# Where twelve table scatters and four operand subtractions stand in an attention stage with routing

## The chip, the cores and the metric

The kernel runs on one core of one Trainium2 chip. The metric is device time in microseconds (us), lower is better. The kernel before took 800.71 us, the median of three runs (800.22 to 800.90). One further execution was profiled; every row below comes from it.

## The reference

Four batches of 768 tokens go through attention with 8 heads of 64 dimensions. Six random projections give each query and key a bucket of 6 bits, and a query sees only keys of its own bucket; where there is none, the masked softmax is uniform. The result is a matrix of 3072 tokens by 512, which a router sends to one of eight experts each.

```python
scores = scale * np.matmul(q, k.transpose(0, 1, 3, 2))
scores = np.where(mask, scores, -1000000000.0)
attn = np.exp(scores - np.max(scores, axis=-1, keepdims=True))
attn = attn / (np.sum(attn, axis=-1, keepdims=True) + 1e-09)
x = np.matmul(attn, v)                       # then (3072, 512)
logits = x @ w_gate + modality_bias[modality_id]
e_idx = np.argmax(logits, axis=1)            # one expert a token
out[mask] = gate_w[mask, None] * (np.maximum(x[mask] @ w1[e], 0.0) @ w2[e])
```

## The kernel before, in words

Attention goes over 16 pairs of heads, four pairs to a batch, numbered 0 to 15. Within a pair there are six steps kt, one for each block of 128 keys. Products run as two float32r matmuls, on a high part and a low part of each operand. For a later pair i the copies `hx` (L161, ScalarE) are the high parts of q (x = 0) and k (x = 1), and one subtraction each (L163) makes the low parts: `b_0` of q and `b_1` of k, 128x768 each. k's low part is made by VectorE; q's is made by GpSimd (POOL), but by VectorE in pairs 9, 10, 13 and 14, which the line RELIEF lists:

```python
lo = nc.vector if i in RELIEF or (x == 1 and i > 1) else nc.gpsimd
```

Both are wanted about two pairs later. On VectorE one of them stands in the last step of pair i-3 or so, ahead of the last reduction of the row maxima (L232). What hangs on that reduction: the maximum `m` (L240, VectorE), its negative `nm` (L242, ScalarE), and its transpose on TensorE (L249), behind which all of TensorE's next work waits, since TensorE works in program order. The transposed maxima lie in PSUM tiles `psx`, of which there are two. VectorE gives one back when it has made `lone` (L252) from it, and then the bucket patterns of the next pair (L207) can be written into it.

GpSimd adds up the exponentials for the row sums: two adds of 128x768 (L302) for each step kt, once ScalarE's second exponential of the step (L299) is done. It also makes `va` (L258 to L260) from the values.

Once the four pairs of a batch are through, the next four pairs carry its routing in small pieces: logits, argmax (`oh`), the rank of each token among its expert's (`rk`), and so each token's row in a table in DRAM (`posi`, six columns of one int32, L615, VectorE). Six indirect DMAs issued by GpSimd (L619) then scatter the records (token, gate weight) of the batch's six token blocks into those rows of `tab`. `posi` is one buffer for all batches. For batch 0 the six scatters are issued in pair 7, for batch 1 in pair 11, for batch 2 in pair 14. Each is placed behind the latest add of GpSimd. In pair 14 the table is first read back (`etb`, L694) for two early expert slots.

Two strings of letters for each step (PLAN) say which piece comes next; TensorE's and SyncE's order is the program's, those of VectorE, ScalarE and GpSimd are made by a scheduler. After pair 15 comes the expert stage, whose work before 520 us belongs partly to the last batch.

Of the kernel before, what the change touches and what calls it, by code (L numbers as in the profile page):

```python
# [19 lines left out]
NT = S // 128  # L20
# [8 lines left out]
LAG = 3  # L29
XAT = (12, 6)  # L30
GAT = ((-13, -10, -7, -4), (-1, -1, -1, -1))
RELIEF = (9, 10, 13, 14)
UPTO = 12
PLAN = (
    "LvSPMSMSfMTfexyhk",
    "SMSMVfSMAAQTeyghk",
    "SMTSMSMlGEfxyk",
    "SMTSMSMAAFGEekk",
    "SMSMTSMgfExehk",
    "SMTSMTSMBAABFGFfFfggehkk",  # L40
)
FIN = (("G", "g", "h", "k"), ("FG", "f", "eE", "eE"))
AHEAD = 2
# [31 lines left out]
    }  # L75


def attention(ctx, actx, tc, a, x_d, route, setup, early_slots, early_tables, latest, adds, bias):
    nc = tc.nc
    v = a["v"]  # L80
    NPR = a.get("npair", NP)
# [6 lines left out]
    ps_x = ctx.enter_context(tc.tile_pool(name="ps_x", bufs=CFG["psx"], space=PSUM))  # L88
# [22 lines left out]
    def load_v(i):  # L111
        b, c = i // 4, i % 4
        t = st[i]
        t["v"] = ldv.tile([P, 2, NT, D], F32, name="vt")
        nc.sync.dma_start(out=t["v"], in_=v[b, 2 * c:2 * c + 2].rearrange("h (p t) d -> p h t d", t=NT))
# [318 lines left out]
    with tc.manual_schedule(engines={mybir.EngineType.PE, mybir.EngineType.SP}):  # L434
        load(1)
        load_v(0)
        load(2)
        load_v(1)
        first_scores = score(0)
        first()  # L440
        wg = sm.tile([P, 4, 8], F32, name="wg", bufs=1)
        nc.sync.dma_start(out=wg, in_=a["moe_w_gate"].rearrange("(c p) e -> p c e", p=P))
        gst = fconst.tile([P, 4, 32], F32, name="gst")
        nc.gpsimd.memset(gst, 0.0)
        nc.gpsimd.tensor_copy(out=gst[0:64, :, 0:8], in_=wg[0:64])
        nc.gpsimd.tensor_copy(out=gst[64:128, :, 16:24], in_=wg[64:128])
        ones = fconst.tile([P, 4, 32], F32, name="ones")
        nc.gpsimd.memset(ones, 0.0)
        for c in range(4):
            nc.gpsimd.memset(ones[:, c, c:c + 1], 1.0)  # L450
        setup()
        avs = weigh()
        fins = xs = ts = iter(())
        for i in range(NPR):
            late = []
            ss = score(i) if i else first_scores
            ms = maxp(i + 1, late) if i + 1 < NPR else iter(())
            last, ts = ts, prep(i + 2) if i + 2 < NPR else iter(())
            if i % 4 == 0 and i > 0:
                fins = finish(i // 4 - 1) if i < NPR - 4 else finish_last()  # L460
            for kt in range(NT):
                for c in (PLAN if i else PLAN0)[kt]:
                    if c == "S":
                        next(ss)
                    elif c == "M":
                        next(ms, None)
                    elif c == "T":
                        next(ts, None)
                    elif c == "P":
                        next(last, None)  # L470
                    elif c == "A":
                        next(avs)
                    elif c == "B":
                        if late:
                            late.pop(0)()
                    elif c == "v":
                        vadds(i)
                    elif c == "V":
                        vsums(i)
                    elif c == "Q":  # L480
                        if i > 0:
                            sums(i - 1)
                    elif c == "L":
                        if i + 3 < NPR:
                            load(i + 3)
                    elif c == "l":
                        if 0 < i < NPR - 1:
                            load_v(i + 1)
                    elif c in FIN[i >= NPR - 4][i % 4]:
                        with tc.issue_after(newest[0]):  # L490
                            next(fins, None)
                    elif c == "x" and i % 4 == 2 or c == "y" and i % 4 == 3:
                        if c == "x" and kt == 0 and i > 4:
                            xs = finish_x(i // 4 - 1, 0, NT)
                        next(xs, None)
                        next(xs, None)
        for _ in avs:
            pass
        sums(NPR - 1)
# [12 lines left out]
EARLYB = 2  # L512
# [17 lines left out]
def router(ctx, tc, a, x_d, tab):  # L530
# [43 lines left out]
            nc.gpsimd.tensor_copy(out=run[0], in_=base)  # L574
            nc.gpsimd.tensor_copy(out=recs[:, :, :, 0], in_=tok)

    scattered, latest, adds = [], [], []

    def route(b, lg, ps):
        l = lg  # L580
        m = wk.tile([P, NT], F32, name="rm")
        nc.vector.tensor_reduce(out=m, in_=l, axis=AX.X, op=ALU.max)
        d = wk.tile([P, NT, E], F32, name="rd")
        nc.vector.tensor_tensor(out=d, in0=l, in1=m.unsqueeze(2).broadcast_to([P, NT, E]), op=ALU.subtract)
        ex = wk.tile([P, NT, E], F32, name="rex")
        nc.scalar.activation(ex, d, AF.Exp)
        yield
        w = wk.tile([P, NT, E], F32, name="rw")
        nc.vector.scalar_tensor_tensor(out=w, in0=d, scalar=0.0, in1=rev.unsqueeze(1).broadcast_to([P, NT, E]), op0=ALU.is_ge, op1=ALU.mult)
        wm = wk.tile([P, NT], F32, name="rwm")  # L590
        nc.vector.tensor_reduce(out=wm, in_=w, axis=AX.X, op=ALU.max)
        oh = wk.tile([P, NT, E], BF16, name="oh")
        nc.vector.tensor_tensor(out=oh, in0=w, in1=wm.unsqueeze(2).broadcast_to([P, NT, E]), op=ALU.is_equal)
        yield
        pp = ps.tile([P, HALF], F32, name="psx")
        for j in range(NT):
            lhs = tri if j == 0 else onesb
            nc.tensor.matmul(pp[:, j * E:NT * E], lhs, oh[:, 0:NT - j].rearrange("p t e -> p (t e)"), start=(j == 0), stop=False, skip_group_check=True)
        for j in range(NT):
            nc.tensor.matmul(pp[:, 64:64 + E], onesb, oh[:, j], start=False, stop=(j == NT - 1), skip_group_check=True)  # L600
        rk = wk.tile([P, NT, E], F32, name="rk")
        nc.vector.tensor_tensor(out=rk, in0=pp[:, 0:NT * E].rearrange("p (t e) -> p t e", e=E), in1=run[b % 2].unsqueeze(1).broadcast_to([P, NT, E]), op=ALU.add)
        nc.vector.tensor_tensor(out=run[(b + 1) % 2], in0=run[b % 2], in1=pp[:, 64:64 + E], op=ALU.add)
        yield
        rec = recs[:, b]
        sm = wk.tile([P, NT], F32, name="rsum")
        nc.vector.tensor_reduce(out=sm, in_=ex, axis=AX.X, op=ALU.add)
        nc.vector.tensor_scalar(out=sm, in0=sm, scalar1=1e-9, scalar2=None, op0=ALU.add)
        nc.vector.reciprocal(rec[:, :, 1].bitcast(F32), sm)
        yield  # L610
        nc.vector.tensor_tensor(out=rk, in0=rk, in1=oh, op=ALU.mult)
        pos = wk.tile([P, NT], F32, name="pos")
        nc.vector.tensor_reduce(out=pos, in_=rk, axis=AX.X, op=ALU.add)
        posi = wk.tile([P, NT], I32, name="posi")
        nc.vector.tensor_copy(out=posi, in_=pos)  # L615
        yield
        for t in range(NT):
            with tc.issue_after(latest[0]) if b < B - 1 else nullcontext():
                ins = nc.gpsimd.indirect_dma_start(out=tab, out_offset=bass.IndirectOffsetOnAxis(ap=posi[:, t:t + 1], axis=0), in_=rec[:, t], in_offset=None).ins  # L619
            for other in scattered:  # L620
                tc.declare_no_dep(ins, other, reason="every token has its own row of the table")
            scattered.append(ins)
            if b < B - 1:
                yield

# [62 lines left out]
    ete = const.tile([P, EARLY, TG, 2], I32, name="ete")  # L688

    def early_tables():  # L690
        for j in range(EARLY):
            o = nc.values_load(eslot[0:1, 1, j:j + 1], engines=[mybir.EngineType.SP], min_val=0, max_val=DUMMY,
                               skip_runtime_bounds_check_because="the on-chip slot table ends with the dummy block")
            nc.sync.dma_start(out=etb[:, j], in_=tab[bass.ds(o, TS), :].rearrange("(p a) w -> p a w", a=TG))  # L694
# [24 lines left out]
        nc.vector.tensor_copy(out=tot[:, 2:3], in_=over[:, 0:1])  # L719
        return big, sml, tot  # L720

    return route, early_slots, early_tables, (eslot, etb, ete), late_slots, setup, latest, adds, bias


def experts(ctx, tc, a, x_d, tab, out, ps_x, ident, first, adds):
# [247 lines left out]
def body(tc, a, out):  # L973
# [1 line left out]
    x_d = tc.dram_tile([N + 1, DM], F32, name="x_d")  # L975
    tab = tc.dram_tile([DUMMY + TS, 2], I32, name="tab")
    with ExitStack() as ctx, ExitStack() as actx:
        route, early_slots, early_tables, early_tiles, late_slots, setup, latest, adds, bias = router(ctx, tc, a, x_d, tab)
        finish, finish_x, ps_x, ident = attention(ctx, actx, tc, a, x_d, route, setup, early_slots, early_tables, latest, adds, bias)
        actx.close()  # L980
        runner, tabs, conditional = experts(ctx, tc, a, x_d, tab, out, ps_x, ident, early_tiles, adds)
        r = runner()
# [38 lines left out]
```

## Time and profile before

| what | value |
|---|---|
| timed runs | 800.22, 800.71, 800.90 us |
| profiled execution | 798.11 us, its span 796.3 us |
| TensorE busy | 748.0 us, 94% of the span |
| VectorE, ScalarE, GpSimd busy | 505.0, 413.6, 438.9 us |
| attention, pairs 0 to 15 | until about 485 us |

The span is what the profile shows between the first and the last instruction; the rest, 1.8 us, lies around it. A row of the timeline has start and duration in us, engine, line, operation, what is written and read, its shape, how often it came in a row, and in brackets how long the engine sat idle before it and who ended that. A duration contains what an instruction waits inside itself, for a port for instance. A row of the windows has the stretch, its length, busy time and number of instructions of each engine, TensorE's granted clock (1.00 is 2.4 GHz, 0.50 is 1.2 GHz), the DMA share and GB/s.

### The profile page before, as it was taken

The numbers are of one execution on the slowest core, as the hardware profiler recorded it, in microseconds if no ns is written. First come the engines' busy times: TensorE is split into PE (matmuls) and PEld (weight loads), VectorE is DVE, ScalarE is ACT, GpSimd is POOL, SyncE is SP. The second block draws the span as 40 slices with busy tenths as digits, with TensorE's granted clock in tenths as the row PEclk, the third lists the DMA queues.
The fourth block names the chain that finished last, engine by engine and source line by source line (L and its number), as shares of the span: only waits on it lengthen the run. The fifth ranks groups of instructions, "written<-read, shape, count | busy, mean of one in ns | idle before, by whom it ended". The sixth has DMA issues, their size and how long they took to land.

```text
span 796.3 us, 11626 instructions
## 1 busy us (share of the span) xinstructions
PE 748.0 (94%) x4060; PEld 522.6 (66%) x4060; DVE 505.0 (63%) x839; ACT 413.6 (52%) x730; POOL 438.9 (55%) x321
## 2 busy tenths in 40 slices
PE   4799999999999999997899899999999999999996
PEld 1555556566655566654555555888888888888885
DVE  5777677587787769778769859764244342752422
ACT  3566666666557566664446455324253334633323
POOL 7198988788779978697857694034220204202002
PEclk9999999999999999999999999999999999999999
DMA  6665544254347524465310276466443535833321
GB/s 204 154 179 159 159 119 129 71 159 113 103 123 160 136 83 117 126 153 121 93 48 14 63 161 218 155 90 229 132 159 86 165 101 173 278 134 123 130 54 60
DMA packets 59572, 104.24 MB, mean 131 GB/s; under 512 B 9709, under 2 KB 30829, under 8 KB 59504
## 3 DMA queue, kind: packets, MB, share of 16 engines
q1 hardware_dynamic: 53424, 88.23, 40.0%
q0 software_dynamic: 4928, 13.14, 5.1%
q10 hardware_dynamic: 1152, 2.03, 0.9%
q8 instruction: 34, 0.56, 0.3%
q14 instruction: 34, 0.28, 0.1%
HBM read 59.89 MB, written 13.33 MB: 92 GB/s over the span
## 4 chain that ended last, share of the span: by engine, by line
PE 68%; DVE 11%; issue 10%; ACT 6%; DMA 2%; SPq 1%; POOL 1%; POOLq 0%; ACTq 0%; DVEq 0%
PE psu L326 12%; PE pss L280 8%; PE pss L281 6%; PE hps L812 5%; PE hps L813 5%; PE hps L811 5%; PE yps L857 4%; PE yps L855 4%; PE yps L856 4%; PE psm L224 4%; ACT pb L292 3%; PE psm L230 2%; DVE mx L226 1%; DVE a_0g L251 1%; PE psx L344 1%
## 5 line engine op out<-in xcount | busy, mean ns | idle before, releaser
L302 POOL TENSOR_TENSOR sp<-sp,pb 128x768 f32<-128x768 f32 x124 | 230.9, 1887 | 35.6 <-ACT pb L299 32.2
L292 ACT ACTIVATE pb<-pss 128x512 f32<-128x512 f32 x192 | 113.8, 598 | 104.8 <-PE pss L281 89.4
L226 DVE TENSOR_REDUCE mx<-psm 128x1 f32<-128x512 f32 x192 | 130.7, 687 | 55.2 <-PE psm L224 54.2
L764 DVE TENSOR_TENSOR w<-raw,w 128x1024 fp32r<-128x1024 f32 x64 | 79.5, 1249 | 94.9 <-ACT w L762 66.5
L326 PE MATMUL psu<-pb,vt 128*64 128x512 f32 (+1 forms) x768 | 134.4, 492 | 0.0
L762 ACT CAST w<-raw 128x1024 fp32r<-128x1024 f32 x64 | 66.9, 1050 | 73.8 <-PE yps L857 62.4
L326 PEld LDWEIGHTS psu<-pb,vt 128*64 128x64 f32 x768 | 50.8, 136 | 69.1 <-issue 58.8
L782 POOL DMA_INDIRECT xg<-x_d,tb x18 | 21.9, 1219 | 117.7 <-DMA tb<-tab 113.4
L280 PE MATMUL pss<-a_0g 128*128 128x512 f32 x192 | 80.4, 419 | 3.5 <-ACT pb L292 2.2
L855 PE MATMUL yps<-w,hl 128*128 128x512 f32 x208 | 82.7, 398 | 0.0
L302 POOL TENSOR_TENSOR sp<-pb,pb 128x768 f32<-128x768 f32 x31 | 58.9, 1918 | 41.0 <-ACT pb L299 40.9
L857 PE MATMUL yps<-w,hh 128*128 128x512 f32 x208 | 81.3, 391 | 0.0
L856 PE MATMUL yps<-w,hh 128*128 128x512 f32 x208 | 81.0, 389 | 0.0
L812 PE MATMUL hps<-xl,w 128*128 128x512 f32 x192 | 74.8, 390 | 1.4 <-DVE xl L801 1.4
L811 PE MATMUL hps<-xh,w 128*128 128x512 f32 x192 | 75.5, 393 | 0.0
L813 PE MATMUL hps<-xh,w 128*128 128x512 f32 x192 | 74.8, 390 | 0.0
L232 DVE TENSOR_REDUCE mx<-psm 128x2 f32<-128x512 f32 x96 | 66.1, 689 | 9.6 <-PE psm L230 7.4
L280 PE MATMUL pss<-a_1g 128*128 128x512 f32 x192 | 68.3, 356 | 3.7 <-ACT pb L299 3.4
L817 ACT ACTIVATE hh<-hps 128x512 fp32r<-128x512 f32 x48 | 28.7, 598 | 74.0 <-PE hps L813 71.8
L281 PE MATMUL pss<-b_0g 128*128 128x512 f32 x192 | 65.9, 343 | 0.0
L281 PE MATMUL pss<-b_1g 128*128 128x512 f32 x192 | 65.7, 342 | 0.0
L818 DVE SCALAR_TENSOR_TENSOR hl<-hps,hh 128x512 fp32r<-128x512 f32 x48 | 33.0, 688 | 51.1 <-ACT hh L817 50.5
(203 smaller groups left out, 1374.3 us busy)
## 6 DMA issues: line engine op xcount, KB each, us to landing
raw<-moe_w SPq DMA_DIRECT2D x64, 512.0 KB
xt<-qk SPq DMA_DIRECT2D x31, 384.0 KB
vt<-v SPq DMA_DIRECT2D x16, 384.0 KB
a_0g<-hx SPq DMA_DIRECT2D x30, 192.0 KB
a_1g<-hx SPq DMA_DIRECT2D x30, 192.0 KB
x_d<-xs SPq DMA_DIRECT2D x18, 256.0 KB
b_1g<-a_1g SPq DMA_DIRECT2D x17, 192.0 KB
b_0g<-a_0g SPq DMA_DIRECT2D x17, 192.0 KB
```

The costliest lines, as they stand in the source:

```text
L226: newest[:] = [nc.vector.tensor_reduce(out=mx[:, qt + j, 1 - h, 0:1], in_=mp, axis=AX.X, op=ALU.max).ins]
L280: nc.tensor.matmul(out, t["s1"][h][:, ks], t["m1"][h][:, cs], start=True, stop=False)
L281: nc.tensor.matmul(out, t["s2"][h][:, ks], t["m2"][h][:, cs], start=False, stop=True)
L292: nc.scalar.activation(t["pb"][kt][:, h, 0:MAIN], sp, AF.Exp, scale=0.125)
L302: add = (nc.vector if h and i in CFG["spd"] else nc.gpsimd).tensor_tensor(out=t["sp"][:, h], in0=(t["pb"][0] if kt == 1 else t["sp"])[:, h ...
L326: nc.tensor.matmul(t["u"][part][64 * h:64 * h + 64, 0:w], t["v"][:, h, kt], t["pb"][kt][:, h, COLS[part]], start=False, stop=(kt == NT - 1 ...
L811: nc.tensor.matmul(hps, lo[:, c, fs], xh[:, c], start=(c == 0), stop=False)
L812: nc.tensor.matmul(hps, hi[:, c, fs], xl[:, c], start=False, stop=False)
L813: nc.tensor.matmul(hps, hi[:, c, fs], xh[:, c], start=False, stop=(c == 3))
L855: nc.tensor.matmul(yps[g], hl[fc][:, gs], hi[:, fb], start=(fc == 0), stop=False)
L856: nc.tensor.matmul(yps[g], hh[fc][:, gs], lo[:, fb], start=False, stop=False)
L857: nc.tensor.matmul(yps[g], hh[fc][:, gs], hi[:, fb], start=False, stop=(fc == 7))
```

## The change

RELIEF is emptied, so that GpSimd makes q's low part in pairs 9, 10, 13 and 14 too. The six scatters of batches 0 and 1 are no longer issued by the routing itself. They are put on a list, and a new letter s in the plan issues one: in steps kt 1, 4 and, for the last pair of a batch only, 5; not in the third pair of a batch (i % 4 is 2). For batch 0 that is kt 4 and 5 of pair 7, kt 1 and 4 of pair 8, kt 1 and 4 of pair 9; for batch 1 the same in pairs 11, 12 and 13. Batches 2 and 3 are left as they were.

```diff
-RELIEF = (9, 10, 13, 14)
+RELIEF = ()
 PLAN = (
     "LvSPMSMSfMTfexyhk",
-    "SMSMVfSMAAQTeyghk",
+    "SMSMVfSMAAQTesyghk",
...
-    "SMSMTSMgfExehk",
-    "SMTSMTSMBAABFGFfFfggehkk",
+    "SMSMTSMgfExeshk",
+    "SMTSMTSMBAABFGFfFfggehksk",
 )
...
+                    elif c == "s":
+                        if later and i % 4 != 2 and (kt < NT - 1 or i % 4 == 3):
+                            later.pop(0)()
...
-        for t in range(NT):
+
+        def put(t):
             with tc.issue_after(latest[0]) if b < B - 1 else nullcontext():
                 ins = nc.gpsimd.indirect_dma_start(out=tab, ...).ins
...
+        puts = [partial(put, t) for t in range(NT)]
+        if b < EARLYB:
+            later.extend(puts)
+            return
+        for p in puts:
+            p()
             if b < B - 1:
                 yield
...
     def early_tables():
+        assert not later
```

The order of TensorE and of SyncE is the same before and after. On the others the pieces below show what stands where.

GpSimd, before, from the second step of pair 11 to the first of pair 12. `pb_...` are the five buffers of exponentials, `tab<-recs,posi` is a scatter:

```order
L302 TENSOR_TENSOR sp<-sp,pb_163 128x768 x2
L619 DMA tab<-recs,posi 25088x2
L302 TENSOR_TENSOR sp<-sp,pb_164 128x768 x2
L619 DMA tab<-recs,posi 25088x2 x2
L302 TENSOR_TENSOR sp<-sp,pb_160 128x768 x2
L619 DMA tab<-recs,posi 25088x2
L302 TENSOR_TENSOR sp<-sp,pb_161 128x768 x2
L619 DMA tab<-recs,posi 25088x2
L302 TENSOR_TENSOR sp<-pb_162,pb_163 128x768 x2
```

The same stretch in the changed kernel:

```order
L302 TENSOR_TENSOR sp<-sp,pb_163 128x768 x2
L302 TENSOR_TENSOR sp<-sp,pb_164 128x768 x2
L302 TENSOR_TENSOR sp<-sp,pb_160 128x768 x2
L623 DMA tab<-recs,posi 25088x2
L163 TENSOR_TENSOR b_0g_115<-xt,hx 128x768
L302 TENSOR_TENSOR sp<-sp,pb_161 128x768 x2
L623 DMA tab<-recs,posi 25088x2
L302 TENSOR_TENSOR sp<-pb_162,pb_163 128x768 x2
```

The scatters ahead of and between the adds of kt 2 to 4 are gone; the first one now stands behind the add of kt 4 (`pb_160`), and behind it q's low part of pair 14.

VectorE, before, in the last step of pair 11 and on to the row sums of pair 12 (L349), the two low parts of pair 14:

```order
L163 TENSOR_TENSOR b_0g_115<-xt,hx 128x768
L232 TENSOR_REDUCE mx<-psm 128x2
L251 SCALAR_TENSOR_TENSOR a_0g_120<-psx,a_0g_120 64x512
L240 TENSOR_REDUCE m_3823<-mx 128x4
L251 SCALAR_TENSOR_TENSOR a_1g_121<-psx,a_1g_121 64x512
L252 TENSOR_SCALAR lone<-psx 128x512
...
L232 TENSOR_REDUCE mx<-psm 128x2
L163 TENSOR_TENSOR b_1g_116<-xt,hx 128x768
L349 TENSOR_TENSOR gs<-gs,psx 128x384
```

The same in the changed kernel:

```order
L163 TENSOR_TENSOR b_1g_116<-xt,hx 128x768
L232 TENSOR_REDUCE mx<-psm 128x2
L251 SCALAR_TENSOR_TENSOR a_0g_120<-psx,a_0g_120 64x512
L240 TENSOR_REDUCE m_3819<-mx 128x4
L251 SCALAR_TENSOR_TENSOR a_1g_121<-psx,a_1g_121 64x512
L252 TENSOR_SCALAR lone<-psx 128x512
...
L232 TENSOR_REDUCE mx<-psm 128x2
L349 TENSOR_TENSOR gs<-gs,psx 128x384
```

The place ahead of L232 is not emptied: k's low part has moved up into it, and the one ahead of L349 is gone. It is the same in pairs 6, 7 and 10.

VectorE, before, at the end of pair 13, where the table rows of batch 2 (`posi`) are made:

```order
L226 TENSOR_REDUCE mx<-psm 128x1
L615 CAST posi<-pos 128x6
L232 TENSOR_REDUCE mx<-psm 128x2
L251 SCALAR_TENSOR_TENSOR a_0g_113<-psx,a_0g_113 64x512
L240 TENSOR_REDUCE m_4433<-mx 128x4
L251 SCALAR_TENSOR_TENSOR a_1g_114<-psx,a_1g_114 64x512
L252 TENSOR_SCALAR lone<-psx 128x512
```

The same in the changed kernel:

```order
L226 TENSOR_REDUCE mx<-psm 128x1
L232 TENSOR_REDUCE mx<-psm 128x2
L251 SCALAR_TENSOR_TENSOR a_0g_113<-psx,a_0g_113 64x512
L240 TENSOR_REDUCE m_4433<-mx 128x4
L251 SCALAR_TENSOR_TENSOR a_1g_114<-psx,a_1g_114 64x512
L618 CAST posi<-pos 128x6
L252 TENSOR_SCALAR lone<-psx 128x512
```

The cast stands four places later, just ahead of the `lone` that gives a `psx` tile back. It overwrites the `posi` that batch 1's scatters read, so it waits until those have landed; the last of them is now issued in step 4 of pair 13.

## Rows read from the trace of the kernel before

**Rows 1.** Page, part 1: busy time, share of the span, instructions of each engine.

```profile
PE 748.0 (94%) x4060; PEld 522.6 (66%) x4060; DVE 505.0 (63%) x839; ACT 413.6 (52%) x730; POOL 438.9 (55%) x321
```

**Rows 2.** Windows: from pair 7's row sums to pair 8's; pair 11's to 12's.

```profile
228.70:255.70 27.00, 26.42 (x160) 16.50 (x158) 20.75 (x35) 17.71 (x35) 25.61 (x18) 1.00 0.71 159
...
340.90:372.90 32.00, 27.76 (x160) 17.55 (x158) 25.29 (x35) 17.38 (x34) 26.99 (x20) 0.95 0.55 134
```

**Rows 3.** Timeline of TensorE: four instructions in pairs 6, 11, 12 and 13.

```profile
219.96 0.37 PE L249 MATMUL psx<-identr,nm 128*128 128x128 f32 x2 [1.15 <-ACT nm L242]
...
363.58 0.37 PE L249 MATMUL psx<-identr,nm 128*128 128x128 f32 x2 [3.79 <-DMA b_0g<-hx]
...
397.78 0.32 PE L207 MATMUL psx<-bits,pat 128*128 128x384 bf16 x1 [1.28 <-DVE gl L386]
...
426.66 0.34 PE L207 MATMUL psx<-bits,pat 128*128 128x384 bf16 x1
```

**Rows 4.** Timeline of ScalarE in the last steps of pair 11.

```profile
354.27 0.60 ACT L299 ACTIVATE pb<-pss 128x512 f32<-128x512 f32 x1
...
363.11 0.41 ACT L242 ACTIVATE nm<-m 128x256 fp32r<-128x256 f32 x1 [4.67 <-DVE m L240]
```

**Rows 5.** Timeline of VectorE: the subtraction ahead of L232 in pairs 6, 7, 11, 12.

```profile
215.53 2.40 DVE L163 TENSOR_TENSOR b_0g<-xt,hx 128x768 fp32r<-128x768 f32 x1
...
244.15 0.95 DVE L163 TENSOR_TENSOR b_0g<-xt,hx 128x768 fp32r<-128x768 f32 x1
...
356.53 5.03 DVE L163 TENSOR_TENSOR b_0g<-xt,hx 128x768 fp32r<-128x768 f32 x1
...
390.38 1.04 DVE L163 TENSOR_TENSOR b_1g<-xt,hx 128x768 fp32r<-128x768 f32 x1
```

**Rows 6.** Timeline of GpSimd at those four places and in pair 13.

```profile
213.49 3.62 POOL L302 TENSOR_TENSOR sp<-sp,pb 128x768 f32<-128x768 f32 x2 [1.77 <-ACT pb L299]
...
244.20 1.73 POOL L619 DMA_INDIRECT tab<-recs,posi  x1 [0.31 <-issue]
...
356.19 0.96 POOL L619 DMA_INDIRECT tab<-recs,posi  x1 [0.30 <-issue]
357.17 3.57 POOL L302 TENSOR_TENSOR sp<-sp,pb 128x768 f32<-128x768 f32 x2
...
388.76 4.33 POOL L302 TENSOR_TENSOR sp<-sp,pb 128x768 f32<-128x768 f32 x2 [3.55 <-ACT pb L299]
393.06 1.81 POOL L163 TENSOR_TENSOR b_0g<-xt,hx 128x768 fp32r<-128x768 f32 x1
394.83 3.58 POOL L302 TENSOR_TENSOR sp<-sp,pb 128x768 f32<-128x768 f32 x2
...
421.21 7.21 POOL L302 TENSOR_TENSOR sp<-sp,pb 128x768 f32<-128x768 f32 x4 [0.62 <-ACT pb L299]
```

**Rows 7.** Windows: behind two idle stretches of TensorE, and end of pair 13.

```profile
363.50:368.00 4.50, 4.42 (x17) 3.55 (x18) 3.47 (x8) 2.36 (x6) 3.54 (x3) 0.62 0.46 128
...
398.00:402.00 4.00, 4.00 (x15) 3.43 (x15) 3.17 (x6) 2.30 (x5) 1.42 (x2) 0.57 0.45 110
...
423.00:431.00 8.00, 7.19 (x44) 4.62 (x43) 7.48 (x18) 4.83 (x11) 5.42 (x4) 1.00 0.00 1
```

**Rows 8.** Timeline of VectorE in pairs 12 and 13.

```profile
395.40 1.31 DVE L372 SCALAR_TENSOR_TENSOR rin<-rin 128x48 f32<-128x48 f32 x1
...
425.25 0.67 DVE L252 TENSOR_SCALAR lone<-psx 128x512 fp32r<-128x512 f32 x1
```

**Rows 9.** Timeline of GpSimd and SyncE: batch 3's last scatter, and the read behind it.

```profile
524.41 1.36 POOL L619 DMA_INDIRECT tab<-recs,posi  x1 [0.30 <-issue]
...
537.86 0.42 SPq L777 DMA_DIRECT2D tb<-tab  x1
```

**Rows 10.** Timeline of SyncE and VectorE: two early table reads and their first use.

```profile
447.12 1.23 SPq L694 DMA_DIRECT2D etb<-tab  x2
...
449.64 0.17 DVE L771 SCALAR_TENSOR_TENSOR ete<-etb 128x8 int32<-128x8 int32 x1 [0.27 <-DMA etb<-tab]
```

More of the change, by code (lines that the diff above doesn't have):

```diff
@@ L75, in host_layout, with attention @@
     }
-def attention(ctx, actx, tc, a, x_d, route, setup, early_slots, early_tables, latest, adds, bias):
+def attention(ctx, actx, tc, a, x_d, route, setup, early_slots, early_tables, latest, adds, bias, later):
     nc = tc.nc
@@ L575, in setup @@
             nc.gpsimd.tensor_copy(out=recs[:, :, :, 0], in_=tok)
-    scattered, latest, adds = [], [], []
+    scattered, latest, adds, later = [], [], [], []
     def route(b, lg, ps):
@@ L720, in late_slots @@
         return big, sml, tot
-    return route, early_slots, early_tables, (eslot, etb, ete), late_slots, setup, latest, adds, bias
+    return route, early_slots, early_tables, (eslot, etb, ete), late_slots, setup, latest, adds, bias, later
 def experts(ctx, tc, a, x_d, tab, out, ps_x, ident, first, adds):
@@ L977, in body @@
     with ExitStack() as ctx, ExitStack() as actx:
-        route, early_slots, early_tables, early_tiles, late_slots, setup, latest, adds, bias = router(ctx, tc, a, x_d, tab)
-        finish, finish_x, ps_x, ident = attention(ctx, actx, tc, a, x_d, route, setup, early_slots, early_tables, latest, adds, bias)
+        route, early_slots, early_tables, early_tiles, late_slots, setup, latest, adds, bias, later = router(ctx, tc, a, x_d, tab)
+        finish, finish_x, ps_x, ident = attention(ctx, actx, tc, a, x_d, route, setup, early_slots, early_tables, latest, adds, bias, later)
         actx.close()
```

## Prediction

> **What bounds the kernel now.** The busy times come first: TensorE is busy for 748.0 of 796.3 us [rows 1], so what another engine gains or loses counts only where TensorE waits for it. Then the windows, cut at the row sums of each pair, so that pairs of the same kind can be laid side by side. Pairs 7 and 11 do the same work, 160 groups of matmuls each, yet the one takes 27.00 us and the other 32.00, at a granted clock of 1.00 and 0.95 [rows 2]. Those 5.0 us are the largest single thing in the attention stage that is not matmul work. The timeline of TensorE names where they are: 3.79 us of idle time ahead of the transpose L249 [rows 3]. The bracket puts it down to a DMA into `b_0`, which that matmul does not read. What it reads is `nm`, which ScalarE began at 363.11 after 4.67 us of waiting for VectorE's maximum [rows 4], and VectorE had been in one subtraction, q's low part of pair 14, from 356.53 on, for 5.03 us [rows 5]. The subtraction itself takes 0.95 us where nothing hinders it, as in pair 7. The rest is a wait for GpSimd: when it starts, GpSimd is in a scatter, goes from there without a gap into two adds until 360.74, and VectorE ends 0.82 us after that [rows 5, 6]. Behind the idle time TensorE got a clock of 0.62 on average for 4.5 us, part of it at the lower of its levels [rows 7]; that costs 0.38 x 4.5 = 1.7 us. Idle time and clock make 5.5 us of the stretch, less some waits elsewhere that pair 7 has and pair 11 lacks; I keep the measured difference, 5.0.
>
> **What GpSimd and VectorE do to each other.** Four places show it [rows 5, 6]. In pair 12 the subtraction starts 1.62 us after GpSimd's first add and takes 1.04: it gets in when the first add ends, and the second waits, so that the two take 4.33 instead of 3.6. In pair 6 it starts 2.04 us after the first add, inside the second, and takes 2.40: it waits for that one to end. In pair 7 it starts 0.05 us ahead of a scatter, does not wait, and the scatter takes 1.73 instead of 0.96. In pair 11 it starts 0.34 us into a scatter and loses to it and to both adds. TensorE's wait follows the subtraction: 1.15 us idle for 2.40, 3.79 for 5.03 [rows 3, 5], so idle time begins when it takes more than about 1.25 us.
>
> **The change part by part.** *The four subtractions that leave VectorE.* They cost GpSimd 4 x 1.81 = 7.2 us [rows 6]. But the place ahead of L232 is not freed, as k's low part moves into it with the same shape, so VectorE's own 0.95 us stay on TensorE's path, and what it sheds is the later subtraction ahead of L349, which nobody waits for. So the four moves by themselves are worth about nothing.
>
> *Pairs 7 and 11, the scatters gone from in front.* What matters is what GpSimd is doing when the subtraction comes. The adds of kt 2 and 3 follow each other without scatters, so GpSimd is free when ScalarE ends the exponential L299 at 354.27 + 0.60 = 354.87 [rows 4]. The adds start about 0.1 us later, 355.0; the first ends at 356.8. VectorE comes at 356.53, as its own queue has not changed ahead of it. It then waits 0.3 us for the first add, as in pair 12, and takes about 1.2 us, under the 1.25 where TensorE starts to wait. The scatter now stands behind the adds. So pair 11 should take pair 7's 27.0 us: 5.0 us gained. Pair 7's subtraction goes from 0.95 to some 1.2: nothing.
>
> *Pairs 6 and 10.* No scatter was there. VectorE comes inside the second add, as before, but GpSimd now has q's low part queued right behind that add. VectorE asked first, and should go first: 2.40 us as before, no change. If GpSimd went first, VectorE would take 2.40 + 1.81 (a rival below). The Trainium skill bears on it (SBUF — State Buffer, "Who interferes with whom"): the port pair shared by the two is an exclusive lock, held for a whole instruction by whoever issued first. By that rule no change here, and the rows of pairs 6 and 12 agree with it (2.40 and 1.04 us); pair 11's 5.03, where VectorE was passed by two adds after the scatter, does not, and so the rival keeps a chance.
>
> *Pair 12.* VectorE's L372 (128x48) takes 1.31 us because it starts inside a GpSimd add that began at 394.83 [rows 6, 8], and the 1.28 us that TensorE waits at 397.78 hang on it [rows 3]. In the changed kernel a scatter (0.96 us and gaps of about 0.2) stands ahead of q's low part there, so at the same moment GpSimd is in the low part, from 394.25 until 396.05, not in an add until 396.64. L372 ends some 0.5 us earlier: 0.5 gained. Behind these waits the clock fell too, 0.57 over 4.0 us, 1.7 us lost [rows 7]. With 0.5 less idle time it may or may not fall; the nearest rows are 1.15 us of idle time without a fall and this one with it, so half: 0.85.
>
> *Pair 13, the wait that is added.* The cast of batch 2's `posi` waits for the landing of batch 1's last scatter. That is issued behind the adds of kt 4, which are the first two of four from 421.21 on, so at about 425.0 [rows 6]. The cast stands behind VectorE's second L251, which ends when L252 starts now, 425.25 [rows 8]; behind it in VectorE's queue is L252, which frees the `psx` tile for TensorE's L207, now at 426.66 without any wait [rows 3]. How long does a scatter take to land? The rows do not show it alone. From below: two small table reads, issued until 448.35, were used at 449.64, 1.3 us after the last issue and 2.5 after the first [rows 10]. From above: the read behind batch 3's last scatter was issued 537.86 - 524.41 = 13.5 us after it [rows 9], in a stretch full of weight loads. At the end of pair 13 the DMA engines are idle, share 0.00 [rows 7], so I take 2.0. Then the cast ends at 425.0 + 2.0 + 0.2 = 427.2, L252 at 427.9, and L207 starts 1.3 us late: 1.3 lost (nothing if the landing takes under 0.7, 12.6 and a fall of the clock, 14.3, at 13.5). The page DMA: Bandwidth & Descriptors of the Trainium skill ("Anatomy of one DMA — SWDGE (gpsimd) path") fits such a DMA by 2.0 us plus bytes over 436e3; that estimate, about 2.0 for 1 KB, would give the same 1.3, and no row here shows it.
>
> *The other scatters* (0.96 us each) go behind adds in pairs 8, 9, 12, 13, where GpSimd has idle stretches (3.55 us ahead of 388.76, [rows 6]) and its results are read a pair later; nothing.
>
> **The sum,** against the profiled execution: 5.0 + 0.5 + 0.85 - 1.3 = 5.05 gained of 798.11 (span 796.3 and 1.8 around it), which gives 793.1. The timed runs lie 2.6 above it, and what differs in them is not shown; the same gain from their median gives **800.71 - 5.05 = 795.7**.
>
> **The rivals.** *The stall is not what the timed runs have.* It hangs on 0.05 us in pair 7 and 0.34 in pair 11. If neither pair stalls in the timed runs, 5.0 of the gain is absent: 800.7. If both do, another 5.0 comes: 790.7. For the second speaks that they are slower than the profiled one, against it that it is by 2.6 and not 5.
>
> *The added wait is long, and the kernel slower.* Place: the cast at the end of pair 13. Without it the gain is 6.35; slower by over 0.2% (1.6 us) needs a loss of 7.95, of which a fall of the clock gives 1.7, so L207 late by 6.25, which is a landing of about 7 us. At 13.5 the loss is 14.3 and the time 808.7. For it: the only row of a scatter's landing is this long; against it: idle DMA engines. Between 4 and 7 us of landing the time ends within 0.2%.
>
> *VectorE comes a little late in pairs 7 and 11,* after the first add has ended. Then it waits for the second, takes 2.40 as in pair 6, and TensorE 1.15 in each: 795.7 + 2.3 = 798.0. It has 0.3 us to spare.
>
> *GpSimd goes first in pairs 6 and 10.* 1.81 us more in each, and perhaps a fall of the clock of 1.7 in each: 795.7 + 3.6 to 7.0 = 799.3 to 802.7.
>
> **Chances and range.** Less than 0.2% (1.6 us) either way cannot be told from no change. My forecast 0.58, by itself 793.5 to 797.5 (the clock of pair 12 either way, the landing between 1.3 and 2.5); neither stall 0.08; both 0.10; long landing 0.12, half of it slower, a quarter the same, a quarter still faster; late in pairs 7 and 11 0.07; GpSimd first 0.05, of which 0.03 slower and 0.02 the same. Faster 0.58 + 0.10 + 0.07 + 0.03 = 0.78; same 0.08 + 0.03 + 0.02 = 0.13; slower 0.09. The range 790.0 to 800.4 leaves out the slower cases and most of "neither".
>
> **What would show it.** Right: the windows from row sums to row sums give about 27 us for pair 11 as for pair 7, k's low part in both takes 1.0 to 1.25 us, 2.40 in pairs 6 and 10, no idle time ahead of L249 in pair 11 and no fall of the clock behind it; L372 under 0.9; the cast of `posi` in pair 13 or the idle time in front of it at about 2 us, and 1.3 us of TensorE waiting ahead of L207. Wrong: a subtraction of over 2 us in pairs 7 or 11, over 4 in pairs 6 or 10, or a wait of more than 4 us at the cast.

## The result, and the profile after

The changed kernel takes 804.17 us (median of seven runs, 802.44 to 806.41) against 799.24 for the kernel before (seven runs, 797.89 to 800.90): a ratio of 1.0057, 95% interval 1.0038 to 1.0076. It is slower; the forecast was 795.7. The profiled execution took 802.92 us (span 801.1), 4.8 above that of before, so the traces show what the timed runs measure.

The windows of the kernel after, from row sums to row sums, for pairs 7, 11, 12, 13 and 14, and then three stretches inside pairs 12, 13 and 14:

```profile
228.29:255.30 27.01, 26.48 (x161) 16.50 (x159) 19.44 (x33) 19.28 (x37) 23.00 (x16) 1.00 0.59 168
341.30:368.31 27.01, 26.49 (x161) 16.51 (x159) 19.45 (x33) 19.29 (x37) 23.03 (x16) 1.00 0.60 171
368.31:407.31 39.00, 30.80 (x190) 18.91 (x188) 27.75 (x47) 16.83 (x35) 27.37 (x21) 0.91 0.26 68
407.31:439.26 31.95, 28.15 (x156) 18.14 (x154) 22.26 (x51) 16.59 (x33) 21.79 (x16) 0.89 0.07 22
439.26:468.38 29.12, 26.17 (x144) 15.85 (x143) 21.52 (x38) 12.84 (x25) 21.47 (x15) 0.94 0.39 109
394.00:401.00 7.00, 4.48 (x15) 3.78 (x15) 5.67 (x10) 2.22 (x5) 1.37 (x2) 0.52 0.22 56
428.00:435.00 7.00, 5.63 (x19) 4.95 (x20) 5.56 (x16) 2.50 (x5) 0.68 (x1) 0.51 0.00 0
448.50:452.00 3.50, 3.50 (x12) 1.22 (x10) 2.24 (x7) 0.63 (x1) 1.77 (x2) 0.51 0.00 0
```

And those of the kernel before for pairs 12, 13 and 14 (pairs 7 and 11 are [rows 2]):

```profile
372.92:408.19 35.27, 30.61 (x189) 18.62 (x187) 24.39 (x48) 18.38 (x37) 25.04 (x18) 0.95 0.33 85
408.19:435.33 27.14, 25.94 (x156) 16.12 (x154) 22.51 (x47) 16.36 (x33) 20.07 (x14) 1.00 0.08 26
435.33:462.82 27.49, 24.64 (x144) 15.40 (x142) 22.32 (x41) 12.82 (x25) 19.93 (x14) 1.00 0.38 112
```

Pair 11 gave the 5.0 us that were forecast: 27.01 us, the same as pair 7, at a full clock. Pair 12 took 3.7 us more than before, pair 13 another 4.8, pair 14 another 1.6. The other pairs from 6 on, pair 10 first, add 0.9 in sum.

The timeline of the kernel after, VectorE and GpSimd in pairs 11 and 12, TensorE in pair 12, and the end of pair 13:

```profile
355.23 4.33 POOL L302 TENSOR_TENSOR sp<-sp,pb 128x768 f32<-128x768 f32 x2 [1.39 <-ACT pb L299]
356.85 1.04 DVE L163 TENSOR_TENSOR b_1g<-xt,hx 128x768 fp32r<-128x768 f32 x1
...
388.09 0.98 POOL L623 DMA_INDIRECT tab<-recs,posi  x1 [0.15 <-issue]
389.11 1.82 POOL L163 TENSOR_TENSOR b_0g<-xt,hx 128x768 fp32r<-128x768 f32 x1
389.56 0.42 DVE L251 SCALAR_TENSOR_TENSOR a_1g<-psx,a_1g 64x256 fp32r<-64x256 f32 x1
390.23 5.22 DVE L372 SCALAR_TENSOR_TENSOR rin<-rin 128x48 f32<-128x48 f32 x1
390.87 3.56 POOL L302 TENSOR_TENSOR sp<-sp,pb 128x768 f32<-128x768 f32 x2
394.39 0.98 POOL L258 TENSOR_TENSOR va<-vt 128x384 f32<-128x384 f32 x1
396.52 0.48 PE L207 MATMUL psx<-bits,pat 128*128 128x384 bf16 x1 [5.20 <-DVE gl L386]
...
424.09 0.98 POOL L623 DMA_INDIRECT tab<-recs,posi  x1
428.35 0.37 DVE L618 CAST posi<-pos 128x6 int32<-128x6 f32 x1 [3.89 <-DMA tab<-recs,posi]
429.37 0.50 PE L207 MATMUL psx<-bits,pat 128*128 128x384 bf16 x1 [3.41 <-DVE lone L252]
```

In pair 11 k's low part comes inside the first add, takes 1.04 us, and the two adds take 4.33, as in pair 12 before [rows 5, 6]. In pair 12 the small instruction L372, 1.31 us in [rows 8], takes 5.22. It came 1.2 us behind the end of a scatter and stayed until GpSimd had gone through q's low part, two adds and `va` (394.39 + 0.98 = 395.37; L372 ends at 395.45). TensorE sat idle for 5.20 us where it was 1.28 in [rows 3], and then ran at about half clock (0.52 over 7 us). In pair 13 the cast of `posi` waited 3.89 us for the scatter in front, TensorE 3.41 for `lone` behind the cast, and again the clock was half (0.51 over 7 us). The cast began 4.26 us after the scatter's start (424.09); the scatter's release of `posi` stands in the trace at 428.06, 4.0 us after that start. The DMA engines were idle in that stretch (share 0.01 or less), so I take the 4.0 us as the scatter's own time to land and not as a queue.

### The profile page after: what moved, and what is told of

Its sections match the earlier page's. It is cut to its first block, busy times and chain, and to the rows that moved or that the text cites. A ratio compares the mean times of both kernels' runs of the same rounds, so it can differ in the third digit from the quotient of the medians.

```text
span 801.1 us, 11630 instructions
## 1 busy us (share of the span) xinstructions
PE 750.5 (94%) x4060; PEld 523.3 (65%) x4060; DVE 497.3 (62%) x835; ACT 414.3 (52%) x730; POOL 445.2 (56%) x325
## 4 chain that ended last, share of the span: by engine, by line
PE 65%; DVE 14%; issue 10%; ACT 5%; DMA 3%; POOL 1%; SPq 1%; POOLq 0%; ACTq 0%; DVEq 0%
PE psu L326 11%; PE pss L280 8%; PE pss L281 6%; PE hps L823 4%; PE hps L825 4%; PE hps L824 4%; PE yps L869 4%; PE yps L867 4%; PE yps L868 4%; PE psm L224 4%; PE psm L230 2%; ACT pb L292 2%; DVE mx L226 2%; DVE b_1g L163 2%; DVE a_0g L251 1%
## 5 line engine op out<-in xcount | busy, mean ns | idle before, releaser
L326 PE MATMUL psu<-pb,vt 128*64 128x512 f32 (+1 forms) x768 | 136.1, 497 | 0.0
L302 POOL TENSOR_TENSOR sp<-pb,pb 128x768 f32<-128x768 f32 x31 | 56.7, 1852 | 30.1 <-ACT pb L299 30.0
L232 DVE TENSOR_REDUCE mx<-psm 128x2 f32<-128x512 f32 x96 | 66.2, 689 | 8.8 <-PE psm L230 6.5
```

The lines of the kernel that those rows point to most:

```text
L302: add = (nc.vector if h and i in CFG["spd"] else nc.gpsimd).tensor_tensor(out=t["sp"][:, h], in0=(t["pb"][0] if kt == 1 else t["sp"])[:, h ...
L326: nc.tensor.matmul(t["u"][part][64 * h:64 * h + 64, 0:w], t["v"][:, h, kt], t["pb"][kt][:, h, COLS[part]], start=False, stop=(kt == NT - 1 ...
```

## The experiments

Theory A: a VectorE instruction that has only SBUF operands, and comes while GpSimd is in an unbroken run that a scatter began, is held until that run breaks; without the scatter it gets in at the end of GpSimd's instruction. The rest of the loss is the cast's wait. Theory B: it is the new load on GpSimd (q's low parts, a longer run of adds) that holds VectorE.

**One part of the change at a time.** `e1_low_parts_only` is the kernel before with one line changed, `e2_scatters_only` the changed kernel with that line put back:

```diff
 e1:
-RELIEF = (9, 10, 13, 14)
+RELIEF = ()
 e2:
-RELIEF = ()
+RELIEF = (9, 10, 13, 14)
```

> The kernel before with q's low parts on GpSimd in pairs 10 and 14 as well; the scatters stay in pairs of two where they were. Theory A (what held VectorE for 5 us is a GpSimd run that begins with a scatter): k's low part in pair 11 stays at about 5 us and the pair at about 32 us, pair 12 stays at about 35 us with the row-index instruction at about 1.3 us, pair 13 at about 27 us since no converted position waits for a scatter; the time is that of before, 799.2 us, within 1.5 us. Rival B (q's low parts on GpSimd are what made pair 12 late): pair 12 comes out at 38 to 39 us and the time near 803 us, 0.4 to 0.5% above before. Both leave pair 13 alone.

> The changed kernel with q's low parts of pairs 9, 10, 13 and 14 where they were before; the single scatters stay. Theory A: pair 11 is 27.0 us (5 us below before), pair 12 about 39 us with the row-index instruction at about 5 us, pair 13 about 32 us behind the wait of the converted positions, so all of the change's loss stays: 803 to 805 us. Rival B: pair 12 falls back to about 35.3 us, and the time to about 800.4 us.

The scatters alone gave 804.66 us, a ratio of 1.0053 (1.0035 to 1.0071): all of the loss, with pair 11 at 27.41, pair 12 at 39.43, pair 13 at 31.93, as theory A had it. The low parts alone gave 804.05, 1.0051 (1.0035 to 1.0067), which neither theory expected: pair 12 took 33.69 us and pair 13 27.43, so q's low parts do not make these pairs late, and in pair 11 k's low part took 4.90 us and the pair 32.96, but pair 7 now stalled as pair 11 does (31.98 us). The timeline of e1 in pair 7:

```profile
244.14 0.96 POOL L619 DMA_INDIRECT tab<-recs,posi  x1 [0.30 <-issue]
244.48 5.05 DVE L163 TENSOR_TENSOR b_1g<-xt,hx 128x768 fp32r<-128x768 f32 x1
245.13 3.58 POOL L302 TENSOR_TENSOR sp<-sp,pb 128x768 f32<-128x768 f32 x2
248.87 1.52 POOL L619 DMA_INDIRECT tab<-recs,posi  x1 [0.17 <-issue]
```

Before, VectorE came 0.05 us ahead of that scatter and was served at once [rows 5, 6]; here it came 0.34 behind and was held for the scatter and both adds. So a shift of 0.4 us between two engines costs 5 us, and 1.04 us of VectorE's work became 5.05.

**The wait of the cast.** `e3_two_posi` is the changed kernel with

```diff
-        posi = wk.tile([P, NT], I32, name="posi")
+        posi = wk.tile([P, NT], I32, name="posi", bufs=2)
```

> The changed kernel with two buffers for the converted positions, so that batch 2's conversion waits for no scatter of batch 1. Theory A (the wait for the last scatter's landing costs 3.4 us of TensorE's time in pair 13 and the half clock behind it another 1.4 us): TensorE's 3.41 us of idle time at the routing sum and the 6.8 us at half clock are gone, pair 13 is about 27.2 us, the time 799.4 us, 4.8 us below the changed kernel and level with before. Rival (pair 13 is late because GpSimd's adds and q's low part came to lie otherwise): pair 13 stays at 30 to 32 us and the time at 802.5 to 804.2 us. In both pair 12 stays at about 39 us.

It took 801.1 us, 1.0011 (0.9994 to 1.0029): of the 4.8 us expected, 3.1 came. The idle time at L207 and the half clock behind it are gone, but a new hold stands behind them, and pair 13 took 29.69 us. The timeline of e3 at the end of pair 13:

```profile
424.13 0.98 POOL L623 DMA_INDIRECT tab<-recs,posi  x1
425.14 3.62 POOL L302 TENSOR_TENSOR sp<-sp,pb 128x768 f32<-128x768 f32 x2
426.60 2.29 DVE L641 TENSOR_TENSOR sg<-run,kstep 128x96 f32<-128x96 f32 x1
429.55 0.51 PE L230 MATMUL psm<-a_0g 128*128 128x256 f32 x2 [2.02 <-DVE mx L226]
```

L641 (1.08 us in the kernel before) came in the run behind the same scatter and ended with it, and TensorE waited 2.02 us. The wait had hidden a hold.

**The scatter of pair 12.** From here on the steps at which a scatter is issued are listed, as they are in the changed kernel but for what is named. In `e4_pair12_moved` (12, 4) becomes (12, 2); `e6_add_in_place` does that too and puts an unused GpSimd add in the scatter's old place.

```diff
-                        if later and i % 4 != 2 and (kt < NT - 1 or i % 4 == 3):
+                        if (i, kt) in SPOTS:
 e6 besides:
+                        if (i, kt) == (12, 4):
+                            with tc.issue_after(latest[0]):
+                                wide = ident.unsqueeze(1).broadcast_to([P, 3, P])
+                                nc.gpsimd.tensor_tensor(out=filler, in0=wide, in1=wide, op=ALU.add)
```

> The changed kernel with the second scatter of pair 12 issued two steps earlier, so that two pairs of adds lie between it and the stretch in which the row-index instruction comes. Theory A (a VectorE instruction that comes in an unbroken GpSimd run behind a scatter is held until that run breaks): the row-index instruction takes about 1.3 us as before (0.7 to 2.4), TensorE's 5.20 us of idle time ahead of the routing's next matmul falls to about 1.3 us, pair 12 is about 35.3 us, the time 800.4 us, 3.7 us below the changed kernel. Rival B (GpSimd's run of adds with q's low part in it is long enough to hold it, with or without a scatter in front): the instruction still takes 4 to 5 us, pair 12 stays at 38 to 39 us, and the time at about 804 us. Pair 13 stays at about 32 us in both.

> The changed kernel with the second scatter of pair 12 issued two steps earlier, and in its old place a GpSimd addition of about 1 us (128 x 384, its result is not used), so that GpSimd's run there has the length and the start that it had with the scatter. Theory A (it is the scatter at the run's head that makes the run hold VectorE): the row-index instruction takes 0.4 to 2 us and pair 12 stays at 33.6 to 35.3 us; the time is about 799.5 us. Rival (a run of that length, begun at that time, holds VectorE whatever stands at its head): the instruction takes 4 to 5.2 us, pair 12 is 37.5 to 39 us, the time about 803 us.

e4 took 798.45 us, 0.9992 (0.9974 to 1.0010), 2.0 better than expected, as no half clock was left in pair 12 (33.60 us); e6 797.41, 0.9983 (0.9970 to 0.9995), pair 12 at 32.69. The window of pair 12 in e4, then the timelines, first e4, then e6:

```profile
369.06:402.66 33.60, 29.14 (x189) 17.40 (x187) 23.58 (x47) 16.71 (x35) 27.43 (x21) 1.00 0.32 80
```

```profile
388.64 1.81 POOL L164 TENSOR_TENSOR b_0g<-xt,hx 128x768 fp32r<-128x768 f32 x1
390.40 3.59 POOL L303 TENSOR_TENSOR sp<-sp,pb 128x768 f32<-128x768 f32 x2
390.98 1.31 DVE L373 SCALAR_TENSOR_TENSOR rin<-rin 128x48 f32<-128x48 f32 x1
393.36 0.32 PE L208 MATMUL psx<-bits,pat 128*128 128x384 bf16 x1 [1.28 <-DVE gl L387]
```

```profile
388.67 0.83 POOL L497 TENSOR_TENSOR filler<-ident 128x384 f32<-128x384 f32 x1
389.45 1.81 POOL L165 TENSOR_TENSOR b_0g<-xt,hx 128x768 fp32r<-128x768 f32 x1
391.01 0.31 DVE L374 SCALAR_TENSOR_TENSOR rin<-rin 128x48 f32<-128x48 f32 x1
391.21 3.62 POOL L304 TENSOR_TENSOR sp<-sp,pb 128x768 f32<-128x768 f32 x2
```

The same instruction, inside the same adds and low part but with no scatter ahead of them, gets in at the end of the GpSimd instruction that it meets, though both runs (from about 384.4 on without a gap) are longer than the changed kernel's. Theory B falls: it is the scatter at the head.

**A pause behind the scatter.** In `e7_scatter_ahead` (7, 4) and (11, 4) become (7, 3) and (11, 3), which puts the scatter ahead of the adds that k's low part meets.

> The changed kernel with the first scatter of pairs 7 and 11 issued a step earlier, some 3 us ahead of k's low part on VectorE; GpSimd pauses for about 0.4 us behind it, since the next addition waits for ScalarE. Theory A (a hold ends with the first pause of GpSimd): k's low part takes about 1.04 us in both pairs, pairs 7 and 11 stay at 27.0 us. Rival 1 (VectorE is held until the scatter has landed, some 4 us after its issue, or to the next instruction boundary after that): 1.5 to 3.5 us in both pairs. Rival 2 (every addition within a few us behind a scatter holds VectorE, pause or not): 3 us or more, and pairs 7 and 11 at about 30 us.

One run, 805.87 us (pairs 12 and 13 lose as in the changed kernel). Timeline in pair 11:

```profile
357.24 0.99 POOL L624 DMA_INDIRECT tab<-recs,posi  x1 [0.15 <-DVE mx L227]
358.69 4.33 POOL L303 TENSOR_TENSOR sp<-sp,pb 128x768 f32<-128x768 f32 x2 [0.47 <-ACT pb L300]
360.30 1.05 DVE L164 TENSOR_TENSOR b_1g<-xt,hx 128x768 fp32r<-128x768 f32 x1
```

With 0.47 us of pause behind the scatter, VectorE 3.1 us after its start is not held, though by the 4.0 us measured above it had not landed; in pair 7 the same (1.05 us), with a pause of 0.07. Behind the scatters that held VectorE, GpSimd's next instruction followed within 0.04 us. So it is not the landing that holds. That it is the pause and not the distance is not quite shown: these two came 2.8 and 3.1 us behind the scatter's start, the held ones 0.3 to 2.5.

**Both repairs.** `e5_both` has the two buffers of e3 and moves (9, 4), (12, 4), (13, 4) to steps 2; `e5b_posi_and_12` has the two buffers and moves (12, 4) alone; `e8_end_of_run` is e5b with (13, 4) moved to (13, 5), the end of GpSimd's run; `e9_end_vector_low` is e8 with RELIEF as before the change. The list of e8, against the changed kernel's steps written as a list:

```diff
-SPOTS = ((7, 4), (7, 5), (8, 1), (8, 4), (9, 1), (9, 4), (11, 4), (11, 5), (12, 1), (12, 4), (13, 1), (13, 4))
+SPOTS = ((7, 4), (7, 5), (8, 1), (8, 4), (9, 1), (9, 4), (11, 4), (11, 5), (12, 1), (12, 2), (13, 1), (13, 5))
```

> The changed kernel with two buffers for the converted positions and with the second scatter of the 9th, 12th and 13th pair issued two steps earlier, so that no scatter begins the GpSimd run in which the routing's VectorE instructions come. Theory A (each loss is a GpSimd run behind a scatter that holds VectorE, plus one wait for a landing): the row-index instruction of pair 12 takes about 1.3 us, no routing instruction of pair 13 takes more than 1.6 us, pair 12 is 33.6 us, pair 13 about 27.2, and the time is 795.5 us, 0.4 to 0.6% below before. Rival (the two repairs do not add: with each taken alone, TensorE's idle time moved on by one stage): the time stays at 798 to 800 us.

> As the kernel sent beside it, but the second scatter of the 9th and of the 13th pair stays where the change put it. Theory A: the scatter of pair 13 again begins the run in which the slot-rank instruction comes, which takes about 2.3 us (1.08 before), and TensorE then idles some 2 us with the half clock behind it: pair 13 is 29 to 30 us, pair 14 29 to 30 us, and the time is 2 to 3 us above the kernel beside it, some 797.5 us. Rival (the 2.3 us have nothing to do with the scatter's place): no difference from the kernel beside it.

e5 missed: 802.6 us, 1.0053 (1.0037 to 1.0069). Pair 12 was repaired (33.66 us), pair 13 took 36.37. Its timeline in pair 13:

```profile
415.26 0.99 POOL L624 DMA_INDIRECT tab<-recs,posi  x1 [0.16 <-issue]
416.28 10.65 POOL L303 TENSOR_TENSOR sp<-sp,pb 128x768 f32<-128x768 f32 x6
417.46 9.53 DVE L615 TENSOR_TENSOR rk<-rk,oh 128x48 f32<-128x48 f32 x1
427.65 0.58 PE L231 MATMUL psm<-a_1g 128*128 128x256 f32 x1 [7.96 <-DVE mx L227]
```

My own repair put the scatter ahead of six adds that follow each other without a break. An instruction of 0.20 us was held for 9.5, past five boundaries, until 426.99, when the last add had ended (426.93). As a test of theory A this says more than the experiment that was meant: the hold has the length of the run. e5b took 796.95 us, 0.9966 (0.9950 to 0.9983); its L642 took 2.27 us behind the scatter and pair 13 29.69, as expected, but pair 14 took 27.54 and not 29 to 30.

> The changed kernel with two buffers for the converted positions, the second scatter of pair 12 two steps earlier, and the second scatter of pair 13 a step later, so that it stands at the end of GpSimd's run of additions, ahead of a pause of several us. Theory A (a scatter harms where it stands at the head of an unbroken run in which VectorE comes, and only there): the slot-rank instruction takes 0.2 to 1.2 us instead of 2.3, no VectorE instruction of pair 13 is held, TensorE's 2 us of idle time in pair 13 falls to about 0.8 as before, pair 13 is about 27.2 us, and the time is about 794.5 us, 0.5 to 0.7% below before. Rival (any scatter in pair 13 holds an instruction of the routing): pair 13 stays at 29 us or more and the time at 797 us or more.

> As the kernel sent beside it, with q's low parts of pairs 9, 10, 13 and 14 back where they were before the change. If those low parts on GpSimd cost time by themselves (pairs 6 and 10 were 0.3 us longer with them): 0.5 to 1 us below the kernel beside it, some 793.8 us. If VectorE's share of them is what they save: pairs 8 and 11 grow by 0.4 to 0.6 us each, and the time is level with or up to 1 us above it. In both, a run of GpSimd that begins with a scatter and meets VectorE may come up by the shift, and would cost 4 to 5 us at that place.

e8 took 796.22 us and its ratio is 0.9913 (0.9890 to 0.9936); the kernel before took 803.19 on that chip, more than elsewhere, which is not explained, so the ratio counts; the profiled spans are 793.8 us here and 796.3 before, 0.3% apart. Windows and timeline of e8, pair 13:

```profile
403.41:430.55 27.14, 25.94 (x157) 16.13 (x155) 21.87 (x47) 16.35 (x33) 22.02 (x16) 1.00 0.09 26
```

```profile
414.57 9.06 POOL L303 TENSOR_TENSOR sp<-sp,pb 128x768 f32<-128x768 f32 x5
422.67 1.07 DVE L642 TENSOR_TENSOR sg<-run,kstep 128x96 f32<-128x96 f32 x1
423.78 0.99 POOL L624 DMA_INDIRECT tab<-recs,posi  x1 [0.15 <-issue]
427.05 0.45 POOL L260 TENSOR_TENSOR va<-va 128x128 f32<-128x128 f32 x1 [2.29 <-PE psx L268]
```

L642 comes in the last of the adds, with no scatter at their head, and takes 1.07 us; pair 13 is back at its 27.14 us. e9 took 796.33, 0.9922 (0.9896 to 0.9949): q's low parts on GpSimd are worth nothing that shows (pair 8 grew by 0.55 us, but pair 11 shrank by 0.6). By the ratios e8 beats both kernels.

## Why the prediction was wrong, point by point

- *Pairs 7 and 11: right.* 27.01 us each, 1.04 us for k's low part, no idle time at L249, no fall of the clock; pair 11 gained the 5.0.
- *The four subtractions worth nothing: right* by e2 beside the whole change, and e9 beside e8. But moving them is not harmless: in e1 it shifted pair 7 into the stall.
- *Pairs 6 and 10: right in mechanism*, 2.30 us for k's low part (2.40). Pair 6 still took 0.3 us more and pair 10 0.94, which no term had. In e3, e5, e5b and e8, which have two `posi` buffers, pair 10 is 28.95 instead of 29.60. The trace shows where the difference lies: at the end of pair 9 two small routing instructions of VectorE (L587, L592) wait for a GpSimd instruction and take 0.85 and 1.44 us (0.20 and 0.50 in e3), the row sums come late, and TensorE waits 0.39 us. Why GpSimd stands otherwise in e3 is open.
- *Pair 12: the step that failed.* "... at the same moment GpSimd is in the low part, ... L372 ends some 0.5 us earlier" took the end of an instruction for the moment at which VectorE gets in. That is so in runs of adds, and I had the counter-example in pair 11, where VectorE was passed by two adds behind a scatter; I took it as a matter of pairs 7 and 11 and did not ask which VectorE instructions would come behind the scatters in their new places: the term "The other scatters ... nothing" looked at GpSimd's idle time and at who reads its results, not at VectorE. What the runs showed in its place is a hold past three boundaries, 5.22 us, and 5.20 us of TensorE's time. Forecast 1.35 gained, measured 3.7 lost. The Trainium skill's rule (SBUF — State Buffer, "Who interferes with whom"), a lock held for one instruction by who issued first, agrees with e4 and e6 (1.31 and 0.31 us); with 5.22 and 9.53 us, three and five boundaries passed, it does not.
- *Pair 13: the mechanism was right, the size was off.* A scatter landed about 4.0 us after its start with idle DMA engines, not 2.0, which was taken from two plain table reads, so L207 waited 3.41 us instead of 1.3, and the clock fell. Together 4.8. The "long landing" rival asked for about 7 us to be slower, since it counted on 1.35 gained in pair 12, where 3.7 were lost. The Trainium skill's fit (DMA: Bandwidth & Descriptors, "Anatomy of one DMA — SWDGE (gpsimd) path") gives 2.0 by estimate; here it was twice that.
- *The clock* had no term behind pair 13 and none in pair 14, where 3.5 us at half clock cost 1.6 though the idle time ahead (2.41 us at L230) is nearly that of before (2.34, no fall). The half given to a fall in pair 12 was a guess between two rows: behind 1.28 us of idle time the clock fell in the kernel before, and in e1 (1.29) and e4 (1.28) it did not. In pair 14 it fell in e1 and e9 (2.34) and not in e5b (2.44) and e8 (2.34). So the length of the idle time alone does not decide; what does is open, and with it the 1.6 us of pair 14.

The sum: -5.0 in pair 11, +3.7 and +4.8 in pairs 12 and 13, +1.6 in pair 14, +0.9 in the other pairs from 6 on: about 6 us later, against which 0.7 had been gained ahead of pair 6 and 0.5 came behind the attention stage. That leaves the 4.8 of the span.

What holds VectorE inside the chip no trace shows. Nor is it settled what ends a hold in each case: in e3 L372 ended at 396.00, with the adds, though `va` followed them within 0.02 us; in the changed kernel it waited for `va` as well.

## What to carry to other kernels

When a GpSimd-issued scatter is moved, look not for idle time in GpSimd but for the VectorE instructions that come between the scatter and GpSimd's next pause: put it at the end of a run, ahead of a wait. An instruction's duration in the trace contains its wait for GpSimd, so a 0.2 us instruction that takes 5 is the row to look for. Buffers read by an asynchronous scatter stay taken until it lands; give the next writer another.

## What the runs showed of the hardware

- VectorE instructions with SBUF operands alone, behind a scatter at the head of an unbroken GpSimd run: 5.05, 5.22, 2.29 and 9.53 us, where the same instructions elsewhere took 0.20 to 1.31; one with a PSUM operand in the same run (L251 at 389.56) took its usual 0.42.
- An indirect scatter of 128 records released its index buffer about 4.0 us after its start, with DMA engines idle.
- TensorE ran at half clock behind 5.20 and 3.41 us of idle time, and behind 2.41 in pair 14; behind 1.28 in e4's pair 12 it did not, though behind 1.28 in the kernel before it did (0.57, [rows 7]).
